# Last two element-wise steps of each spectral product on GpSimd, and a feed that aims eight steps ahead

## The chip, the core and the metric

One core of a Trainium2 chip runs the whole program. The metric is the device time of one execution in microseconds; lower is better. The engines are named as in the profile: PE is TensorE, PEld its weight load, DVE is VectorE, ACT is ScalarE, POOL is GpSimd, SP is SyncE. SP and POOL also issue DMAs, each from its own queue, in the order in which the instructions stand there.

## What is computed

A long convolution per channel, done with Fourier transforms, and a two-layer network on its result, all in float32:

```python
def _attn_ref(x, v, pos_emb, w1, w2):          # x, v: (4, 12480, 128)
    h_filt = (np.maximum(pos_emb @ w1, 0.0) @ w2) * window
    u = x * v
    y = irfft(rfft(u, n=2*S) * rfft(h_filt, n=2*S), n=2*S)[:, :S, :]
    return x * y
def _moe_ref(x, w_in, w_out):                  # x: (49920, 128), w_in: (128, 2048)
    h = x @ w_in
    g = h * (1.0 / (1.0 + np.exp(-1.702 * h)))
    return g @ w_out
```

## The kernel before

**Sets.** The convolution is cut into five sets (a half of the sequence, and one or two batch entries). A set has three phases. Phase 1 (`p1_unit`, 26 units) transforms the products x·v along one axis and stores them in DRAM as `g_d`. Phase 2 (`p2_unit`, 31 units a set, 30 of two columns and a last one of one) loads `g_d`, transforms along the other axis on PE (`forward`, L324, "cv<-g,wf"), multiplies by the filter's spectrum on DVE, transforms back on PE (`inverse`, L330, "ab<-t,wv") and stores `z_d`. Phase 3 (`p3_unit`) is done for each of 104 blocks of 480 columns: it loads `zt` (from `z_d`), `vt` and `x`, makes the last transform on PE (L520, "cv<-vt,zt"), and multiplies by x on DVE (L530 to L541). Set 0 goes through phases 1 and 2 in a start stage of about 200 us.

**The network.** After the start stage the program writes 104 blocks n of 8 steps k, that is 832 steps. A step has six matmuls of 480 columns into `h` (L592), two activations on ACT (L593, L594), one subtraction on DVE (L600, "fgl<-fg,fgh", written at the start of the next step) and six matmuls into `acc` (L609), three steps later. A block's result `ot` is stored from POOL at k = 4 of the next block (L620). At the end of step k = 7 of block n, `p3_unit(n + 2)` is started: its loads (L494 twice, L498, L500) are issued by POOL there, and its matmuls L520 are written at the end of step k = 2 of block n + 1, three steps later.

**The feed.** The phases 1 and 2 of sets 1 to 4 run between the steps. `Feed` holds their units with a weight each (1.4 or 1.6 for phase 1, 2.4 for phase 2) and marks, the summed weight at which a set is complete. After each step `feed.run(1.0)` raises a goal by a rate and lets units run until their weight has reached it. `feed.pace(k, span)` sets the rate to (mark − goal) / span. The rate is set at step 14 (`HOLD`) for set 1, and then at the steps 95, 199 and 407 (`begin`), at which the blocks of a new set are first loaded, for the sets 2, 3 and 4. Blocks 0 to 12 belong to set 0, 13 to 25 to set 1, 26 to 51 to set 2, 52 to 77 to set 3, 78 to 103 to set 4. So set 2 is prepared during the blocks of set 1, and so on; after set 4 is prepared only the network and phase 3 are left.

**The product.** Within a `p2_unit`, `t1` (called `y` in another view, two buffers) and `t2` (`yb`, one buffer) hold the products of the spectrum with the filter's real and imaginary part, in rows of 512 numbers a partition and half (256 in set 1 and in the last unit of a set). The sets 3 and 4 first add an older product (L419 or L423, L441, L443). The last two instructions, L463 and L464, form y = t1 − t2 and y = t1 + t2 on the two halves, in place. `inverse` reads y two or three units later. A `yield` ends a unit's share of one round, a `yield 1` only gives way to the steps.

Of the kernel before, what the change touches and what calls it, by code (L numbers as in the profile page):

```python
# [13 lines left out]
ALU = mybir.AluOpType  # L14
# [24 lines left out]
HOLD = 14  # L39
# [76 lines left out]
def conv_ffn_kernel(  # L116
# [17 lines left out]
    nc = tc.nc  # L134
    act = nc.scalar.activation
    tt = nc.vector.tensor_tensor
# [243 lines left out]
    def spec_store(eu, w0, nw, q=nc.sync):  # L380
        q.dma_start(out=e_d[0][:, w0:w0 + nw], in_=eu[:, 0, 0:nw])
        q.dma_start(out=us_d[0][:, 0, w0:w0 + nw], in_=eu[:, 1, 0:nw])

    def p2_unit(j, v):
# [27 lines left out]
        def tmp(name, bufs):  # L412
            t = sb(name, [128, 1024], F32, bufs)[:, 0:2 * wd]
            return t.rearrange("p (w l c) -> p w l c", w=nw, l=lq), t.rearrange("p (w l c) -> p w l c", w=nw, l=2)
# [19 lines left out]
        t1, y = tmp("t1", 2)  # L434
        t2, yb = tmp("t2", 1)
# [9 lines left out]
        else:  # L445
# [3 lines left out]
            if mixed:  # L449
                e1 = sb("e1", [128, 2, 2, 128], F32, 2)  # L450
                for i in range(2):
                    nc.vector.scalar_tensor_tensor(out=e1[:, 0:nw, i], in0=e0[:, 0:nw, i], scalar=sgn_sb,
                                                   in1=xs[i][:, :, 0], op0=ALU.mult, op1=ALU.add)
# [6 lines left out]
            yield 1  # L460
            tt(out=t2, in0=us[:, 0:nw], in1=both(e0, 1), op=ALU.mult)
            yield 1
        tt(out=y[:, :, 0], in0=y[:, :, 0], in1=yb[:, :, 1], op=ALU.subtract)  # L463
        tt(out=y[:, :, 1], in0=y[:, :, 1], in1=yb[:, :, 0], op=ALU.add)  # L464
        yield
        yield
        z = sb("z", [128, 2, 2, 256], F32, 3, "az")
# [155 lines left out]
    def conv_feed():  # L623
        p1 = {j: [(p1_unit(j, p), 1.6 if j == 1 else 1.4) for p in range(NP)] for j in range(1, 5)}
        ahead = {2: 5, 3: 16, 4: 16}
        units, marks = list(p1[1]), []
        for j in range(1, 5):
            nxt = p1.get(j + 1, [])
            n = ahead.get(j + 1, 0)
            units += nxt[:n]  # L630
            units += [(p2_unit(j, v), 2.4) for v in range(NV)]
            m = 8 if j == 1 else NP - n
            units += nxt[n:n + m]
            if j >= 3:
                units += [(None, 2.0)] * 12
            marks.append(sum(w for _, w in units))
            units += nxt[n + m:]
        return units, marks

    def fill(o, q):  # L640
        d = z_d[o][:, KZ:KP].rearrange("r k (q c) -> r (k q) c", c=128)
        q.dma_start(out=d, in_=zero.unsqueeze(1).broadcast_to([128, d.shape[1], 128]))

    with tc.manual_schedule():
# [48 lines left out]
        def when(n):  # L693
            return (n - 1) * STEPS - 1

        first = {next(i for i, hv in enumerate(HV) if hv[0] == o): o for o in range(1, 5)}
        begin = sorted(when(n) for n in first)
        feed = Feed(pipe, *conv_feed())
        feed.pace(0, begin[0] - HOLD)
        for n in range(7):  # L700
            p3.tick(p3_unit(n // 6) if n in (0, 6) else None)
            if n == 1:
# [8 lines left out]
        for n in range(NH):  # L711
            for k in range(STEPS):
                if pend:
                    ffn.lo(pend[-1])
                if len(pend) == LAG - 1 and pend[0][1] == STEPS - 1:
                    ffn.mm2(pend.pop(0))
                pend.append(ffn.mm1(n, k))
                t = n * STEPS + k
                if t == 1:
                    nc.gpsimd.tensor_tensor(out=sgn0, in0=gate[:, 0:1], in1=gate[:, 0:1], op=ALU.mult)  # L720
                if t == 1 or t == 9:
                    for _ in range(KEEP // 2):
                        spec_store(*spectra.pop(0), nc.gpsimd)
                if t == HOLD:
                    keep_cm.__exit__(None, None, None)
                    for o in range(1, 5):
                        fill(o, nc.gpsimd)
                    ps["s"] = ctx.enter_context(tc.tile_pool(name="main", bufs=1, side="right", reuse_waits="tile"))
                if len(pend) == LAG:
                    ffn.mm2(pend.pop(0))  # L730
                if t >= HOLD:
                    feed.run(1.0)
                new = None
                if k == STEPS - 1 and n + 2 < NH:
                    if n + 2 in first:
                        o = first[n + 2]
                        feed.reach()
                        if o < 4:
                            feed.pace(o, begin[o] - begin[o - 1] - 2)
                        else:  # L740
                            feed.rate = 0.0
                    new = p3_unit(n + 2)
                p3.tick(new)
                if k == 4:
                    ffn.store()
# [127 lines left out]
```

## Time and profile before

| | |
|---|---|
| time of the kernel before, median of 3 runs | 3049.63 us (3048.06 to 3049.92) |
| the profiled execution: its time, its span | 3054.41 us, 3052.6 us |
| mean granted TensorE clock | 0.994 |
| busy share of the span | PE 98%, PEld 77%, DVE 70%, ACT 69%, POOL 15% |
| instructions on POOL | 765 |
| DMA, mean over the span | 178 GB/s |

A row of the profile has line, engine, operation, the tile written and those read, the shapes as partitions × elements, the count, then busy microseconds and the mean time of one in nanoseconds, and then the engine's idle time just before them with what ended it. A row of the timeline has the start, the duration, and the same names. Busy DVE times of neighbours overlap a little: the spacing of starts is what one costs.

### The profile page before, as it was taken

The page shows a single profiled execution, that of the slowest core. Times are in us where ns is not written, and L with a number is a line of the kernel's source. Part 1 is how long each engine was busy: PE and PEld are TensorE (multiplying, and loading weights), DVE is VectorE, ACT ScalarE, POOL GpSimd, SP SyncE. Part 2 cuts the span into 40 slices and gives each one's busy share as a digit, 9 for nine tenths or more (in the row PEclk, how much of TensorE's full clock was granted, in tenths as well). Part 3 has the DMA queues.
Part 4 walks back from the last instruction along what each step waited for, and adds up shares of the span by engine and source line. Part 5 has one row for each costly group of instructions (what it writes and reads, how often), then busy time and mean ns, then how long its engine had stood idle before and what let it go on. Part 6 is the DMA issues. An engine that isn't in the chain of part 4 may idle for free.

```text
span 3052.6 us, 42552 instructions
## 1 busy us (share of the span) xinstructions
PE 2983.5 (98%) x15508; PEld 2349.7 (77%) x15508; DVE 2148.7 (70%) x2909; ACT 2091.3 (69%) x2689; POOL 466.7 (15%) x765
## 2 busy tenths in 40 slices
PE   8899999999999899999999999999999999999999
PEld 4458876688766688777778887777778888888888
DVE  7555677777787667999996469888995454444444
ACT  3456776688777777666668766666667677777676
POOL 2254111022101111101111111111111111111110
PEclk9999999999999999999999999999999999999999
DMA  9879899999788966666566324555541111111110
GB/s 298 265 256 285 243 292 281 290 315 312 248 269 270 277 187 203 200 197 195 189 190 172 112 83 158 170 163 165 177 142 63 57 50 46 60 46 46 60 46 27
DMA packets 261105, 541.88 MB, mean 178 GB/s; under 512 B 30978, under 2 KB 120762, under 8 KB 260898
## 3 DMA queue, kind: packets, MB, share of 16 engines
q1 hardware_dynamic: 205970, 377.29, 38.9%
q0 software_dynamic: 54928, 161.86, 17.7%
q8 instruction: 125, 2.05, 0.3%
q14 instruction: 82, 0.67, 0.1%
HBM read 330.24 MB, written 208.80 MB: 177 GB/s over the span
## 4 chain that ended last, share of the span: by engine, by line
PE 57%; DVE 7%; issue 1%; DMA 1%; ACT 0%; SPq 0%; POOL 0%; DVEq 0%; POOLq 0%
PE h L592 24%; PE acc L609 24%; PE cv L520 4%; DVE fgl L600 2%; PE ab L330 1%; DVE t L423 1%; PE cv L324 1%; DVE t L438 1%; DVE t L439 1%; DVE t L443 1%; PE cv L178 1%; PE cv L180 1%; PE cv L179 1%; DVE t L441 0%; DMA u<-us_d 0%
## 5 line engine op out<-in xcount | busy, mean ns | idle before, releaser
L600 DVE TENSOR_TENSOR fgl<-fg,fgh 128x960 fp32r<-128x960 f32 x832 | 956.9, 1154 | 426.0 <-ACT fg L594 424.3
L593 ACT ACTIVATE fgh<-h 128x960 fp32r<-128x960 f32 x832 | 809.1, 972 | 541.5 <-PE h L592 541.0
L592 PE MATMUL h<-xh,wi 128*128 128x480 f32 x3328 | 1149.4, 386 | 12.6 <-ACT fg L594 11.9
L609 PE MATMUL acc<-fgh,wo 128*128 128x480 f32 x3328 | 866.4, 382 | 0.0
L594 ACT ACTIVATE fg<-h 128x960 f32<-128x960 f32 x832 | 804.3, 967 | 65.3 <-DVE fgl L600 65.0
L592 PEld LDWEIGHTS h<-xh,wi 128*128 128x128 f32 x3328 | 628.0, 189 | 188.6 <-ACT fg L594 37.8
L609 PEld LDWEIGHTS acc<-fgh,wo 128*128 128x128 f32 x3328 | 625.8, 188 | 110.9 <-issue 12.9
L592 PE MATMUL h<-xl,wi 128*128 128x480 f32 x1664 | 634.3, 381 | 2.0 <-DVE xl L541 2.0
L609 PE MATMUL acc<-fgl,wo 128*128 128x480 f32 x1664 | 502.5, 383 | 5.2 <-DVE fgl L600 5.2
L620 POOL DMA_DIRECT2D out_dram<-ot x104 | 57.1, 549 | 1965.6 <-ACT ot L613 1908.9
L609 PEld LDWEIGHTS acc<-fgl,wo 128*128 128x128 f32 x1664 | 312.6, 188 | 57.4 <-DVE fgl L600 7.8
L592 PEld LDWEIGHTS h<-xl,wi 128*128 128x128 f32 x1664 | 313.8, 189 | 50.2 <-DVE xl L541 5.0
L520 PEld LDWEIGHTS cv<-vt,zt 122*128 122x128 f32 x1664 | 203.1, 194 | 28.9 <-issue 16.8
L520 PE MATMUL cv<-vt,zt 122*128 122x120 f32 x1664 | 207.6, 279 | 8.3 <-DMA vt<-in_c_v_dram 6.5
L324 PE MATMUL cv<-g,wf 52*64 52x512 f32 (+1 forms) x1240 | 178.9, 595 | 11.7 <-DMA g<-g_d 6.1
L530 DVE TENSOR_TENSOR a<-cv,yq 128x240 f32<-128x240 f32 (+1 forms) x101 | 40.7, 403 | 209.5 <-ACT yq L528 209.5
L494 POOL DMA_DIRECT2D zt<-z_d x204 | 148.4, 733 | 6.5 <-issue 3.7
L311 ACT ACTIVATE a<-cv 128x512 f32<-128x512 f32 x208 | 121.0, 599 | 17.2 <-PE cv L180 12.8
L473 ACT ACTIVATE z<-ab 128x1024 f32<-128x1024 f32 (+2 forms) x124 | 112.6, 908 | 28.7 <-PE ab L330 24.9
L278 POOL DMA_DIRECT2D ft<-in_c_f_dram x108 | 57.6, 535 | 451.9 <-PE cv L180 431.5
L330 PE MATMUL ab<-t,wv 52*64 52x512 f32 (+2 forms) x992 | 120.5, 556 | 1.2 <-ACT fg L594 1.2
L459 DVE TENSOR_TENSOR t<-us,e 128x512 f32<-128x512 f32 (+2 forms) x62 | 58.5, 944 | 86.3 <-PE ab L330 53.5
(90 smaller groups left out, 2561.9 us busy)
## 6 DMA issues: line engine op xcount, KB each, us to landing
g_d<-a SPq DMA_DIRECT2D x260, 256.0 KB
g<-g_d SPq DMA_DIRECT2D x300, 208.0 KB
zt<-z_d POOLq DMA_DIRECT2D x204, 256.0 KB, 4.7
e<-e_d SPq DMA_DIRECT2D x180, 256.0 KB
z_d<-z SPq DMA_DIRECT2D x90, 512.0 KB
xt<-in_xv_dram SPq DMA_DIRECT2D x78, 480.0 KB
u<-us_d SPq DMA_DIRECT2D x60, 512.0 KB
ft<-in_c_f_dram POOLq DMA_DIRECT2D x108, 240.0 KB, 5.1
```

Source lines behind the costliest of these rows:

```text
L311: act(a[:, ri], b, ACTF.Copy)
L324: mm(out=xy[q ^ c][64 * c:64 * c + 64, 0:256 * nw].rearrange("p (w c) -> p w c", w=nw), lhsT=wf[64 * q:64 * q + N2, c], rhs=g[64 * q:64 * ...
L330: mm(out=ab[h][64 * pl:64 * pl + 64, 0:w].rearrange("p (w c) -> p w c", w=nw), lhsT=wv[64 * h:64 * h + N2, pl], rhs=y[pl ^ h][64 * h:64 * ...
L459: tt(out=t1, in0=us[:, 0:nw], in1=both(e0, 0), op=ALU.mult)
L473: act(zv.rearrange("p w a c -> p a w c"), ab[:, :, 0:wd].rearrange("p a (w c) -> p a w c", w=nw), ACTF.Copy)
L494: q.dma_start(out=zv[:, gq], in_=z_d[o][64 * gq + 2 * p0:64 * gq + 2 * p0 + 2 * npr].rearrange("r k c -> k r c"))
L520: mm(out=b[:, c0:c0 + M], lhsT=lhs, rhs=rhs, start=(k == 0), stop=(k == 1))
L592: mm(out=h[:, i, 0:TW], lhsT=wt[:, s], rhs=xx, start=st, stop=sp)
L593: act(gh, h[:, :, 0:TW], ACTF.Gelu_apprx_sigmoid)
L594: act(gf, h[:, :, 0:TW], ACTF.Gelu_apprx_sigmoid)
L600: tt(out=gl, in0=gf, in1=gh.bitcast(F32), op=ALU.subtract)
L609: mm(out=acc, lhsT=wt[:, 2 * k + i, :], rhs=xx[:, i], start=(t == 0 and i == 0 and k == 0), stop=(t == 2 and i == 1 and k == STEPS - 1))
```

## The change

It moves the two last instructions of the product from VectorE to GpSimd, and it shortens each span over which the feed is paced by six steps, so that a set's mark is aimed at eight steps ahead of the step at which its first block is loaded instead of two (and for set 1 six steps earlier than before).

```diff
         tt(out=t2, in0=us[:, 0:nw], in1=both(e0, 1), op=ALU.mult)
         yield 1
-        tt(out=y[:, :, 0], in0=y[:, :, 0], in1=yb[:, :, 1], op=ALU.subtract)
-        tt(out=y[:, :, 1], in0=y[:, :, 1], in1=yb[:, :, 0], op=ALU.add)
+        pt = nc.gpsimd.tensor_tensor
+        pt(out=y[:, :, 0], in0=y[:, :, 0], in1=yb[:, :, 1], op=ALU.subtract)
+        pt(out=y[:, :, 1], in0=y[:, :, 1], in1=yb[:, :, 0], op=ALU.add)
         yield
...
         feed = Feed(pipe, *conv_feed())
-        feed.pace(0, begin[0] - HOLD)
+        feed.pace(0, begin[0] - HOLD - 6)
...
                         if o < 4:
-                            feed.pace(o, begin[o] - begin[o - 1] - 2)
+                            feed.pace(o, begin[o] - begin[o - 1] - 8)
```

The added line shifts the numbers behind it by one: L463 and L464 become L464 and L465, L494 becomes L495, L600 becomes L601 and so on.

The queue of POOL before, in the middle of set 2's phase 2, holds one block's store and the next but one block's loads, and nothing else:

```order
L500 DMA x_9483<-in_xtm_dram 128x480
L620 DMA out_dram<-ot 128x480
L494 DMA zt<-z_d_81 128x4x128 x2
L498 DMA vt<-in_c_v_dram 128x480
L500 DMA x_9783<-in_xtm_dram 128x480
```

The same place of POOL's queue in the changed kernel:

```order
L621 DMA out_dram<-ot 128x480
L464 TENSOR_TENSOR t_8867<-t_8867,t_8868 128x2x256
L465 TENSOR_TENSOR t_8867<-t_8867,t_8868 128x2x256
L464 TENSOR_TENSOR t_8937<-t_8937,t_8938 128x2x256
L465 TENSOR_TENSOR t_8937<-t_8937,t_8938 128x2x256
L495 DMA zt<-z_d_81 128x4x128 x2
L499 DMA vt<-in_c_v_dram 128x480
L501 DMA x_8978<-in_xtm_dram 128x480
```

Two pairs of the product now stand between the store and the loads, and the pair ahead of the loads reads t_8938, a tile that DVE writes.

The DVE order around that pair in the changed kernel, up to the phase 3 (a_9104) that uses the loads of x_8978:

```order
L459 TENSOR_TENSOR t_8937<-us,e_8793 128x1024
L461 TENSOR_TENSOR t_8938<-us,e_8793 128x1024
L601 TENSOR_TENSOR fgl<-fg,fgh 128x960 x2
L459 TENSOR_TENSOR t_9013<-us,e_8876 128x1024
L461 TENSOR_TENSOR t_9014<-us,e_8876 128x1024
L601 TENSOR_TENSOR fgl<-fg,fgh 128x960
L531 TENSOR_TENSOR a_9104<-cv,yq 128x240
L532 TENSOR_TENSOR a_9104<-cv,yq 128x240
```

Three subtractions of the network, so three steps, lie between t_8938 and L531 (L530 before): the pair is written in the very step at whose end the loads are issued.

In set 3 the DVE order before has L463 and L464 right behind L443, or one subtraction later:

```order
L441 TENSOR_TENSOR t_12442<-t_12442,t_12424 128x1024
L443 TENSOR_TENSOR t_12443<-t_12443,t_12427 128x1024
L463 TENSOR_TENSOR t_12442<-t_12442,t_12443 128x2x256
L464 TENSOR_TENSOR t_12442<-t_12442,t_12443 128x2x256
L600 TENSOR_TENSOR fgl<-fg,fgh 128x960 x2
L423 TENSOR_TENSOR t_12533<-u_12369,e_12367 128x4x128 x2
```

In the changed kernel DVE goes on with the network and the next unit's products:

```order
L441 TENSOR_TENSOR t_12462<-t_12462,t_12444 128x1024
L443 TENSOR_TENSOR t_12463<-t_12463,t_12447 128x1024
L542 TENSOR_TENSOR xl<-a_12397,xh 128x480
L601 TENSOR_TENSOR fgl<-fg,fgh 128x960 x2
L423 TENSOR_TENSOR t_12543<-u_12386,e_12384 128x4x128 x2
```

What follows L443 there reads two tiles in SBUF each time; the instructions that read PSUM (cv) come later.

## The prediction

> **What bounds the kernel now.** I read the page's first part, then windows from store to store in each stage, the groups, and last the timeline of POOL, DVE and PE around one phase 3. The page's first row:
>
> ```profile
> PE 2983.5 (98%) x15508; PEld 2349.7 (77%) x15508; DVE 2148.7 (70%) x2909; ACT 2091.3 (69%) x2689; POOL 466.7 (15%) x765
> ```
>
> PE looks full, but its ends are modelled, so I count blocks. The windows run from one `ot` (L613) to a later one: phase 2 of set 2 (from 829), of set 3 (1207), of set 4 (1830), and after the feed (2392). Columns: window, length, then PE, PEld, DVE, ACT, POOL busy with counts, granted clock, DMA share, GB/s.
>
> ```profile
> 829.40:987.30 157.90, 156.45 (x882) 107.89 (x881) 126.28 (x143) 119.97 (x156) 16.14 (x26) 1.00 0.81 267
> 1206.70:1605.50 398.80, 386.91 (x2064) 292.25 (x2063) 398.05 (x539) 257.13 (x302) 44.93 (x74) 1.00 0.61 193
> 1829.90:2245.60 415.70, 415.70 (x2193) 328.15 (x2192) 376.22 (x446) 282.73 (x331) 48.83 (x80) 1.00 0.51 166
> 2391.95:2801.55 409.60, 409.60 (x2018) 357.04 (x2017) 198.02 (x215) 288.72 (x342) 54.91 (x90) 1.00 0.16 51
> ```
>
> The same windows for L613 alone (both ends counted: blocks are the count less one), then for L330 (eight matmuls a unit):
>
> ```profile
> 829.40:987.30 157.90, 2.81 (x6) 1.00 0.81 267
> 1206.70:1605.50 398.80, 7.96 (x15) 1.00 0.61 193
> 1829.90:2245.60 415.70, 9.18 (x17) 1.00 0.51 166
> 2391.95:2801.55 409.60, 10.29 (x19) 1.00 0.16 51
> ...
> 829.40:987.30 157.90, 21.78 (x160) 4.15 (x160) 1.00 0.81 267
> 1206.70:1605.50 398.80, 32.67 (x240) 6.23 (x240) 1.00 0.61 193
> 1829.90:2245.60 415.70, 27.23 (x200) 5.20 (x200) 1.00 0.51 166
> ```
>
> A block without feed takes 409.60 / 18 = 22.76 us. In set 4, 16 blocks and 25 units take 415.70, so a unit adds (415.70 − 364.1) / 25 = 2.06 us of PE. Set 2 fits: 5 blocks and 20 units, 2.2 us a unit. In set 3, 14 blocks and 30 units should take 318.6 + 61.8 = 380.4 and take 398.8: some 18 us more, 3 of them for phase 1 units at the edges, and DVE is busy for 398.05 of 398.80. So PE is the bound in sets 2 and 4, where DVE has 20% and 9.5% to spare, and DVE in set 3, which costs 15 us. That is all that relief of DVE can bring there.
>
> **Part 1: the two instructions on GpSimd, as DVE sees them.** What leaves DVE, what such work costs on POOL (L365, L366 in the start stage), and what happens when both engines work at once:
>
> ```profile
> L463 DVE TENSOR_TENSOR t<-t,t 128x512 f32<-128x512 f32 x90 | 62.1, 690 | 2.1
> L464 DVE TENSOR_TENSOR t<-t,t 128x512 f32<-128x512 f32 x90 | 61.6, 685 | 0.0
> ...
> 195.29 0.72 POOL L366 TENSOR_TENSOR y<-t,t 128x256 f32<-128x256 f32 x1
> 195.97 0.45 POOL L365 TENSOR_TENSOR y<-t,t 128x128 f32<-128x128 f32 x1
> ...
> 147.98 1.29 DVE L361 TENSOR_TENSOR t<-cv,eu 128x512 f32<-128x512 f32 x2 [1.15 <-PE cv L330]
> 148.05 0.72 POOL L365 TENSOR_TENSOR y<-t,t 128x256 f32<-128x256 f32 x1 [1.02 <-PE cv L330]
> ...
> 165.31 0.68 DVE L564 TENSOR_TENSOR w<-w,w 128x512 uint32<-128x512 uint32 x1
> 165.55 1.01 POOL L365 TENSOR_TENSOR y<-t,t 128x256 f32<-128x256 f32 x1 [1.99 <-DVE t L361]
> 166.02 1.10 DVE L565 TENSOR_TENSOR w<-w,w 128x512 f32<-128x512 f32 x1
> 166.53 1.18 POOL L366 TENSOR_TENSOR y<-t,t 128x256 f32<-128x256 f32 x1
> 167.04 1.22 DVE L566 TENSOR_TENSOR w<-w,wo 128x512 f32<-128x512 f32 x1
> 168.29 0.69 DVE L567 SCALAR_TENSOR_TENSOR wo<-w,w 128x512 fp32r<-128x512 f32 x1
> ```
>
> From 128 to 256 numbers POOL goes from 0.45 to 0.72, so 512 cost about 0.72 + 0.55 = 1.27 us, against 0.69 on DVE. L361 reads PSUM, and neither side slows. L565 and L566 read two tiles in SBUF: they take 1.10 and 1.22 where their like takes 0.69, 0.41 and 0.53 more, while POOL's take 1.01 and 1.18 instead of 0.72. The engines take turns, and a GpSimd instruction of 0.72 us holds DVE up for 0.47. At 1.27 us I estimate 0.47 + 0.55 = 1.0; two a unit, 2.0, less a tenth because L438, L439, L530 and L531 read PSUM: 1.8. Relief is two starts, 1.21 us by the row spacing of L463 and L464 below (913.73 to 914.94). So DVE loses 0.6 us a unit instead of gaining 1.2.
>
> The Trainium skill ("SBUF — State Buffer", sections "SBUF: two separate sides" and "Who interferes with whom") says that GpSimd and a DVE instruction with two SBUF inputs exclude each other for the whole instruction. By that the loss would be 2 × 1.27 less a tenth, 2.3 a unit, and set 3 some 15 us slower than by the rows. The rows agree with the lock, but show it shorter than the instruction.
>
> Set 3 is DVE-bound: 31 × 0.6 = +19 us. Against it, the new pace runs set 3 at 0.625 weight a step instead of 0.642 (the goal has run past the mark by eight steps when the next span begins, so the shorter span is made up for): 2.6% more blocks, 0.4, in the stage, each with 12 us less DVE than PE work (198.02 / 18 = 11.0 against 22.8): −5. **Term 1: +14**, between −15 (no lock, DVE free) and +28 (each delay as long as POOL's 1.27). In sets 2 and 4 the 0.6 is covered by DVE's spare 20% and 9.5% (4 units of 31.6 us: 8%; 1.6 of 26 us: 4%); if that cover goes in set 4, +8, kept for the range.
>
> **Part 2: POOL's queue, where phase 3's loads stand.** Before, POOL waits for `ot`, stores, and goes straight on to the loads; nothing else is there:
>
> ```profile
> 893.39 1.50 POOL L494 DMA_DIRECT2D zt<-z_d  x2
> 894.88 0.55 POOL L498 DMA_DIRECT2D vt<-in_c_v_dram  x1
> ...
> 926.69 2.04 PE L520 MATMUL cv<-vt,zt 122*128 122x120 f32 x16
> ...
> vt<-in_c_v_dram POOLq DMA_DIRECT2D x6, 240.0 KB, 8.3
> ...
> vt<-in_c_v_dram POOLq DMA_DIRECT2D x14, 120.0 KB, 6.0
> ...
> 1059.40 1.47 POOL L494 DMA_DIRECT2D zt<-z_d  x2 [0.27 <-DMA g_d<-a]
> 1060.86 0.56 POOL L498 DMA_DIRECT2D vt<-in_c_v_dram  x1
> 1068.98 3.74 PE L520 MATMUL cv<-vt,zt 122*128 122x120 f32 x16 [4.04 <-DMA vt<-in_c_v_dram]
> ```
>
> vt is issued 31.8 us ahead of its use and lands in 8.3 (set 2; 6.0 in set 3). That lead exists because the loads, written at k = 7, run up to the store of k = 4. Where POOL's queue was held by other work (1059, behind phase 1 loads), vt had 8.1 us, PE stood 4.04 us, and the sixteen L520 then took 3.74 instead of 2.04: 5.7 us in all.
>
> With the change, L464 and L465 of one to three units stand between store and loads, and wait for DVE. The loads can't leave before the last pair is done. The DVE rows around that L520, to place it:
>
> ```profile
> 913.73 0.69 DVE L463 TENSOR_TENSOR t<-t,t 128x512 f32<-128x512 f32 x1
> 914.94 2.22 DVE L600 TENSOR_TENSOR fgl<-fg,fgh 128x960 fp32r<-128x960 f32 x2
> 922.27 1.15 DVE L600 TENSOR_TENSOR fgl<-fg,fgh 128x960 fp32r<-128x960 f32 x1
> 927.17 1.15 DVE L600 TENSOR_TENSOR fgl<-fg,fgh 128x960 fp32r<-128x960 f32 x1
> 930.70 0.40 DVE L530 TENSOR_TENSOR a<-cv,yq 128x240 f32<-128x240 f32 x1
> ```
>
> The loads stand three subtractions ahead of L530, so before the second one of 914.94. In the new order the pair's L459 and L461 come just there, behind the first: they end at about 918. Two GpSimd instructions of 1.27, each waiting for its turn, end at 921; two zt issues, 922.5; vt lands 8.3 later, 931. L520 is due at 926.7: PE stands 4 us, and its slow matmuls add 1.7 as at 1069. By the order of the changed kernel seven blocks of set 2 have the pair in the very step of the loads: 7 × 5.7 = **+40**, between 0 (products 4 us earlier) and +65.
>
> In set 3 three blocks have it in that step, six one step earlier. There:
>
> ```profile
> 1316.50 0.68 DVE L463 TENSOR_TENSOR t<-t,t 128x512 f32<-128x512 f32 x1
> 1322.37 1.94 PE L520 MATMUL cv<-vt,zt 122*128 122x120 f32 x16
> ```
>
> A pair ready at 1316.5 ends at 1320, zt at 1321.5, vt at 1327.5, 5 us after 1322.4; since DVE is the bound and works on behind PE, I take 3.5 of it: 3 × 3.5 = **+10**, and nothing for the others (one step is worth 3.5 us). Set 4: three such blocks, PE-bound, so 3.3 + 1.7 each: **+15**. Set 1 (half-size pairs, five such blocks): 1 us each, **+5**. These two are estimates from set 2's and set 3's rows, between 0 and twice that.
>
> Two waits are new on the tiles. t2 has one buffer, so the next unit's L461 (L439) waits for L465: in set 2 two subtractions and an L459 lie between, some 3.3 us, about what the pair takes, and in set 3 more; 0, or at most 0.5 us a unit in set 2, which PE's bound covers. `inverse` reads y two units later, 15 us in set 2 (31.6 / 4 each): 0.
>
> **Part 3: the earlier goal.** All issues of the units move with it: SP's loads and stores and POOL's ft keep their order among themselves, and the store and load queues see the same bytes. Set 1 runs 8% denser (134.2 weight in 75 steps, not 81). PE bounds that stage too, so the same work only moves: 0, or, if DMA should bound it (share 0.94 there at most), 0.4 of a block, +9. What it can bring is the stand at the end of set 2, where the last units come close together:
>
> ```profile
> 1019.25 0.49 PE L592 MATMUL h<-xh,wi 128*128 128x480 f32 x1 [3.86 <-ACT fg L594]
> ```
>
> With slow matmuls behind it, 1.7 as at 1069, it costs 5.6 us, and the late loads at 1069 another 5.7; at best both go. The units keep their order and only shift against the steps, so I take a third: **−4**, between −11 and 0.
>
> **Sum.** +14 + 40 + 10 + 15 + 5 − 4 = +80. The profiled execution took 3054.41 for a span of 3052.6, 4.8 over the median 3049.63; the terms are differences, so I add them to the median: 3130 us.
>
> **The rivals.**
> 1. POOL's delay is harmless (the products are early enough, or the landing is quicker when the queue is later): terms of part 2 vanish, +10 remain: 3060. For it: the 23 us between landing and use that the loads have before; against it: 1059.40, where the same lateness cost 5.7.
> 2. Faster: the engines hardly meet, because DVE's turns are long and POOL's short. Then set 3 becomes PE-bound, −15, and the stands at 1019 and 1069 go, −11: 3024. It decides if the delay per GpSimd instruction is under 0.6 us and part 2 adds nothing. Against it: L565 and L566.
> 3. The stalls feed on each other: DVE's delay makes the pairs later in set 4 too (four more blocks at 5 us) and set 2 takes its upper 65, set 4 its 8: +80 + 20 + 25 + 8: 3183.
>
> **How the numbers follow.** Forecast 0.58 (own range 3085 to 3170), rival 1 0.20, rival 2 0.10, rival 3 0.12. 0.2% of the time, 6 us, is about what a measurement of this kernel can tell. Slower: the forecast, rival 3 and most of rival 1, 0.85; same, 0.06 from between rivals 1 and 2; faster 0.09. The range leaves out rival 2 and the upper half of rival 3: 3052 to 3180.
>
> **What would show it.** L464 and L465 at about 1.3 us alone and up to 2 with waiting; L601 and L423 of set 3 with maxima near 2 us instead of 1.15 and 0.69; "PE cv L520 <- DMA vt" rising to tens of us; the loads in set 2 at most 12 us ahead of L520. If vt still leads by 20 us, part 2 is wrong; if set 3's blocks fall to 27.2 us, part 1 is.

## The result, and the profile after

| | before | after |
|---|---|---|
| median | 3049.78 us (4 runs) | 3158.80 us (4 runs, 3155.59 to 3164.79) |
| profiled execution: time, span | 3054.41, 3052.6 us | 3155.59, 3153.8 us |
| granted clock, mean | 0.994 | 0.98 |

The ratio is 1.0356 (95% interval 1.0343 to 1.0369): 109 us slower by the medians, 101 by the two profiled executions, from which the tables below are made. The first row of the page after:

```profile
PE 3016.5 (96%) x15508; PEld 2377.1 (75%) x15508; DVE 2144.9 (68%) x2661; ACT 2090.4 (66%) x2689; POOL 925.1 (29%) x1013
```

DVE has 248 instructions fewer and is busy for 3.8 us less (2148.7 before): what left came back as slower instructions. POOL's busy time doubled. The windows of the four stages of the feed show where the time lies. They run from the `ot` of block 0 to that of block 12, and on to the `ot` of blocks 25, 51 and 77, the last of each set; set 1 is prepared in the first, set 2 in the second, set 3 in the third, set 4 in the fourth (each but the last also holds about a block and a half of the next set's feed at its end). The columns are those of the prediction's windows. Before, and then after:

```profile
238.84:667.13 428.29, 419.11 (x2192) 320.91 (x2192) 306.22 (x540) 305.48 (x469) 75.51 (x128) 0.98 0.94 282
667.14:1097.72 430.58, 418.03 (x2178) 315.93 (x2178) 316.73 (x421) 328.30 (x446) 61.03 (x103) 0.98 0.86 270
1097.73:1801.66 703.93, 692.01 (x3559) 555.24 (x3559) 574.37 (x772) 486.78 (x595) 91.13 (x151) 1.00 0.57 174
1801.67:2460.14 658.47, 656.14 (x3409) 528.64 (x3409) 526.53 (x620) 448.62 (x524) 79.35 (x130) 1.00 0.41 134
```

```profile
237.72:684.84 447.12, 430.05 (x2243) 329.25 (x2243) 306.37 (x508) 315.87 (x492) 148.06 (x200) 0.98 0.96 291
684.85:1137.86 453.01, 422.95 (x2157) 321.31 (x2157) 310.30 (x348) 322.86 (x438) 171.96 (x161) 0.96 0.79 250
1137.87:1889.59 751.72, 705.97 (x3546) 564.60 (x3546) 579.13 (x703) 480.76 (x580) 245.04 (x210) 0.97 0.51 158
1889.60:2561.32 671.72, 658.78 (x3393) 532.58 (x3392) 525.09 (x545) 448.90 (x525) 199.96 (x190) 0.99 0.40 127
```

The stages lose 18.8, 22.4, 47.8 and 13.3 us; blocks 78 to 103 take 587.3 us in both. DVE is busy for 579 us in set 3 though 69 instructions fewer lie in that window. The list of waits (in total, times, longest) names what is new:

```profile
POOL t L464 <- DVE t L443: 586.4, 57, 32.9
PE cv L521 <- DMA vt<-in_c_v_dram: 74.6, 26, 7.2
PEld cv L521 <- DMA vt<-in_c_v_dram: 20.7, 5, 7.9
DVE t L439 <- POOL t L465: 13.9, 9, 1.8
```

PE waited 6.5 us in all for `vt` before. The 74.6 are 0.5 us in set 1, 24.9 in set 2, 36.3 in set 3 and 12.9 in set 4. The chain of work around one phase 3 of set 2 shows the step that the prediction worked out (start, duration, what):

```profile
891.97 2.08 POOL t L464
894.05 2.15 POOL t L465
896.20 1.46 POOL zt L495 x2
897.67 4.59 DMA vt<-in_c_v_dram
...
902.39 3.74 PE cv L521 x16
```

The pair takes 4.2 us instead of 2 × 1.25, the loads wait behind it, and `vt` is issued 4.7 us ahead of its use, late as that is, where it had 31.8. The timeline (start, duration, what, and in brackets the wait before) has the stand that follows (PE idle for 4.82 us) in its first row here. The other rows are from set 3, with two pictures of the meeting of the engines: at 1523 they take turns; at 1488 GpSimd ends only after DVE has left a gap:

```profile
902.39 3.74 PE L521 MATMUL cv<-vt,zt 122*128 122x120 f32 x16 [4.82 <-DMA vt<-in_c_v_dram]
...
1488.57 2.21 DVE L601 TENSOR_TENSOR fgl<-fg,fgh 128x960 fp32r<-128x960 f32 x2
1488.82 6.57 POOL L464 TENSOR_TENSOR t<-t,t 128x512 f32<-128x512 f32 x1 [10.45 <-DVE t L443]
1490.70 2.48 DVE L423 TENSOR_TENSOR t<-u,e 128x512 f32<-128x512 f32 x4
1493.11 1.14 DVE L601 TENSOR_TENSOR fgl<-fg,fgh 128x960 fp32r<-128x960 f32 x1
1494.89 0.69 DVE L438 TENSOR_TENSOR t<-cv,e 128x512 f32<-128x512 f32 x1 [0.64 <-PE cv L324]
1495.36 1.25 POOL L465 TENSOR_TENSOR t<-t,t 128x512 f32<-128x512 f32 x1
1496.64 0.69 DVE L439 TENSOR_TENSOR t<-cv,e 128x512 f32<-128x512 f32 x1 [1.05 <-POOL t L465]
1498.01 0.57 POOL L499 DMA_DIRECT2D vt<-in_c_v_dram  x1
1501.83 1.42 PE L521 MATMUL cv<-vt,zt 122*128 122x120 f32 x5 [7.00 <-DMA vt<-in_c_v_dram]
...
1522.80 1.15 DVE L601 TENSOR_TENSOR fgl<-fg,fgh 128x960 fp32r<-128x960 f32 x1
1523.05 2.04 POOL L464 TENSOR_TENSOR t<-t,t 128x512 f32<-128x512 f32 x1 [9.70 <-DVE t L443]
1523.87 2.24 DVE L601 TENSOR_TENSOR fgl<-fg,fgh 128x960 fp32r<-128x960 f32 x1
1525.06 2.20 POOL L465 TENSOR_TENSOR t<-t,t 128x512 f32<-128x512 f32 x1
1526.03 2.25 DVE L601 TENSOR_TENSOR fgl<-fg,fgh 128x960 fp32r<-128x960 f32 x1
...
1551.59 6.59 POOL L464 TENSOR_TENSOR t<-t,t 128x512 f32<-128x512 f32 x1 [11.03 <-PE h L593]
1564.85 3.74 PE L521 MATMUL cv<-vt,zt 122*128 122x120 f32 x16 [4.73 <-DMA vt<-in_c_v_dram]
```

In the case at 1488 PE then stands for 7.00 us, and L439 waits for L465, which still reads the one buffer of t2.

A stand costs more than its own length. The windows of the sixteen L521 behind the stand, and then of a sixteen without one in the kernel before:

```profile
902.39:906.13 3.74, 3.73 (x17) 3.74 (x18) 0.00 (x0) 0.00 (x0) 0.22 (x1) 0.50 0.95 362
```

```profile
926.69:928.73 2.04, 2.04 (x21) 2.04 (x18) 2.04 (x3) 1.96 (x4) 0.91 (x2) 1.00 0.98 289
```

The granted clock is 0.50 in the one and 1.00 in the other. So the 1.7 us that the prediction added to each stand are matmuls at half the clock. Each of the 14 stands of more than 2 us for `vt` in the sets 2 to 4 is followed by a slow sixteen, of 2.34 to 3.77 us.

### The profile page after: what moved, and what is told of

Its sections match the earlier page's. It is cut to its first block, busy times and chain, and to the rows that moved or that the text cites. A ratio compares the mean times of both kernels' runs of the same rounds, so it can differ in the third digit from the quotient of the medians.

```text
span 3153.8 us, 42690 instructions
## 1 busy us (share of the span) xinstructions
PE 3016.5 (96%) x15508; PEld 2377.1 (75%) x15508; DVE 2144.9 (68%) x2661; ACT 2090.4 (66%) x2689; POOL 925.1 (29%) x1013
## 4 chain that ended last, share of the span: by engine, by line
PE 33%; issue 24%; POOL 7%; DVE 7%; DMA 3%; ACT 0%; POOLq 0%; SPq 0%; DVEq 0%
PE h L593 13%; PE acc L610 12%; PE cv L521 4%; DMA vt<-in_c_v_dram 3%; POOL t L464 3%; DVE fgl L601 2%; POOL zt L495 2%; PE ab L330 2%; POOL t L465 1%; PE cv L324 1%; DVE t L438 1%; DVE t L439 1%; DVE t L443 1%; DVE t L423 1%; POOL out_dram L621 1%
## 5 line engine op out<-in xcount | busy, mean ns | idle before, releaser
L601 DVE TENSOR_TENSOR fgl<-fg,fgh 128x960 fp32r<-128x960 f32 x832 | 1050.9, 1269 | 428.5 <-ACT fg L595 422.6
L464 POOL TENSOR_TENSOR t<-t,t 128x512 f32<-128x512 f32 (+2 forms) x124 | 247.4, 1995 | 881.2 <-DVE t L443 586.4
L521 PE MATMUL cv<-vt,zt 122*128 122x120 f32 x1664 | 229.7, 297 | 76.8 <-DMA vt<-in_c_v_dram 74.6
L521 PEld LDWEIGHTS cv<-vt,zt 122*128 122x128 f32 x1664 | 222.7, 211 | 101.1 <-issue 68.0
L531 DVE TENSOR_TENSOR a<-cv,yq 128x240 f32<-128x240 f32 (+1 forms) x101 | 40.7, 403 | 287.1 <-ACT yq L529 287.1
L465 POOL TENSOR_TENSOR t<-t,t 128x512 f32<-128x512 f32 (+2 forms) x124 | 216.0, 1742 | 0.0
L495 POOL DMA_DIRECT2D zt<-z_d x204 | 149.9, 738 | 5.8 <-DMA zt<-z_d 2.8
```

Of the source, the lines that this page charges most:

```text
L464: pt(out=y[:, :, 0], in0=y[:, :, 0], in1=yb[:, :, 1], op=ALU.subtract)
L465: pt(out=y[:, :, 1], in0=y[:, :, 1], in1=yb[:, :, 0], op=ALU.add)
L495: q.dma_start(out=zv[:, gq], in_=z_d[o][64 * gq + 2 * p0:64 * gq + 2 * p0 + 2 * npr].rearrange("r k c -> k r c"))
L521: mm(out=b[:, c0:c0 + M], lhsT=lhs, rhs=rhs, start=(k == 0), stop=(k == 1))
L601: tt(out=gl, in0=gf, in1=gh.bitcast(F32), op=ALU.subtract)
```

## The experiments

"Before" in a ratio is the kernel before on the same chip. Four versions separate the parts first.

**The pace alone.** The changed kernel with the two instructions back on DVE:

```diff
-        pt = nc.gpsimd.tensor_tensor
-        pt(out=y[:, :, 0], in0=y[:, :, 0], in1=yb[:, :, 1], op=ALU.subtract)
-        pt(out=y[:, :, 1], in0=y[:, :, 1], in1=yb[:, :, 0], op=ALU.add)
+        tt(out=y[:, :, 0], in0=y[:, :, 0], in1=yb[:, :, 1], op=ALU.subtract)
+        tt(out=y[:, :, 1], in0=y[:, :, 1], in1=yb[:, :, 0], op=ALU.add)
```

> The changed pace with L463 and L464 left on VectorE. If the GpSimd queue and the shared port make the loss, the pace alone gives 3040 to 3055 us (the stand at the end of set 2 may go, at best 11 us). If the denser feed makes the loss, it gives 3080 or more.

Measured 3066.13 us, ratio 1.0048 (1.0031 to 1.0064), between the two ranges that were expected: a loss of some 15 us where the prediction had a gain. Its windows:

```profile
239.30:696.38 457.08, 432.49 (x2243) 329.03 (x2242) 321.08 (x570) 315.80 (x492) 81.22 (x138) 0.98 0.93 285
696.39:1117.44 421.05, 411.40 (x2157) 309.05 (x2156) 312.83 (x411) 322.56 (x438) 59.01 (x99) 1.00 0.85 268
1117.45:1817.50 700.05, 688.71 (x3546) 551.05 (x3546) 576.37 (x767) 480.87 (x580) 88.40 (x146) 1.00 0.55 169
1817.51:2470.62 653.11, 653.10 (x3393) 528.47 (x3392) 514.51 (x605) 449.00 (x525) 79.47 (x130) 1.00 0.41 131
```

The gains at the end of set 2 and behind are there (−9.5, −3.9, −5.4; block 23 takes 32.9 us instead of 44.0, block 25 28.3 instead of 35.5), but the denser set 1 costs +28.8. PE has 13.4 us more work in that window, which the three later ones are spared (−6.6, −3.3, −3.0), so the work only moves; the other 15.4 us are new idle time of PE, and they make the loss.

**GpSimd alone**, with the old pace:

```diff
-        feed.pace(0, begin[0] - HOLD - 6)
+        feed.pace(0, begin[0] - HOLD)
...
-                            feed.pace(o, begin[o] - begin[o - 1] - 8)
+                            feed.pace(o, begin[o] - begin[o - 1] - 2)
```

> The two instructions on GpSimd with the old pace (two steps ahead). If the loss comes from GpSimd, 3140 to 3170 us, as the whole change, since the pairs still stand between store and loads. If the pace is half of it, about 3100.

3128.85 us, ratio 1.0249 (1.0232 to 1.0266), which is neither of the two times expected. By the ratios the two instructions alone cost 76 us and the pace alone 15; together they cost 109, so some 18 belong to both at once (each of the three is known to 4 or 5 us). PE waits 48.7 us for `vt` here and 74.6 in the change: the pace seems to decide, too, which pairs stand ahead of the loads.

**The loads ahead of the pairs.** The changed kernel with phase 3's loads written at k = 4, right behind the store, and three more yields, so that L521 stays in its step; 3 instead of 6 and 5 instead of 8 in the pace, since `begin` counts from the loads:

```diff
-                if k == STEPS - 1 and n + 2 < NH:
+                if k == 4:
+                    ffn.store()
+                if k == 4 and n + 2 < NH:
...
```

> The whole change, but phase 3's loads are written three steps earlier, at k = 4 right behind the store, so that no pair of k = 5 to 7 stands ahead of them; L521 stays where it is. Queue theory: the waits of PE for vt fall from over 100 us to under 20, and the time to 3060 to 3085; what is left over the twin without GpSimd is what VectorE loses by the shared port, 15 to 30 us. Port theory (VectorE held up is the main loss, the late vt a symptom): 3110 or more.

**Its twin on DVE**, the same without GpSimd's instructions:

> The twin of the one above with L463 and L464 on VectorE: the loads at k = 4, the pace eight steps ahead. 3035 to 3050 us: the loads behind phase 1's ft get three steps more, which can take the stand of 5.7 us at 1069 and a few like it. Its difference to the run above is the price of GpSimd with a free queue.

The first gave 3081.99 us, ratio 1.0098 (1.0082 to 1.0114), 77 less than the change. PE's wait for `vt` is no longer in its list, while L439's wait for L465 is longer:

```profile
DVE t L439 <- POOL t L465: 25.3, 14, 2.1
```

The twin gave 3057.12 us, ratio 1.0017 (1.0006 to 1.0028), slower than the 3035 to 3050 expected. The early loads thus take 9 us off the pace alone, and what GpSimd still costs with its loads out of the way is 25.

**The loads on another queue.** Since the loads at k = 4 also come earlier in the program, a later run left them where the change has them and took them off POOL:

```diff
-        q = nc.gpsimd if n > 1 else nc.sync
+        q = nc.sync
```

> The changed kernel whole, but phase 3's loads (zt, vt, x) are issued by SP at the end of step 7, as late as they are written, so that they no longer stand behind the two GpSimd instructions; POOL keeps the stores. If the loss of 77 us that went with the loads at k = 4 comes from their place in POOL's queue, and not from the later steps of phase 3, most of it goes here too: 3085 to 3110, with the vt waits of PE under 20 us together and a lead of vt near 20 us. Rival: what counts is only how early the loads are written; SP too issues them at k = 7, behind its own loads and stores of the feed, and the time stays at 3140 to 3165.

3089.31 us, ratio 1.0122 (1.0108 to 1.0136): in the first range, so the place in the queue is what costs. Its windows, and from its list of waits the one for `vt`:

```profile
238.54:694.52 455.98, 431.71 (x2243) 331.38 (x2243) 305.78 (x508) 316.21 (x492) 111.39 (x146) 0.97 0.94 285
694.53:1118.76 424.23, 412.31 (x2157) 312.30 (x2157) 310.40 (x349) 322.62 (x438) 138.44 (x109) 0.99 0.84 265
1118.77:1840.31 721.54, 695.54 (x3546) 554.36 (x3545) 575.83 (x703) 480.22 (x580) 196.83 (x106) 0.99 0.53 164
1840.32:2493.42 653.10, 653.09 (x3393) 528.48 (x3392) 526.47 (x545) 448.93 (x525) 135.06 (x86) 1.00 0.41 132
```

```profile
PE cv L521 <- DMA vt<-in_c_v_dram: 14.6, 9, 2.6
```

With these the 102 us of the four windows fall into three parts, each the difference of two of the runs above:

| stage | change − before | pace (pace alone − before) | GpSimd, loads out of its queue (loads on SP − pace alone) | the queue (change − loads on SP) | predicted |
|---|---|---|---|---|---|
| set 1 | +18.8 | +28.8 | −1.1 | −8.9 | +5 |
| set 2 | +22.4 | −9.5 | +3.2 | +28.8 | +40 − 4 |
| set 3 | +47.8 | −3.9 | +21.5 | +30.2 | +19 − 5 + 10 |
| set 4 | +13.3 | −5.4 | 0.0 | +18.6 | +15 |
| sum | +102.3 | +10.0 | +23.6 | +68.7 | +80 |

**What on GpSimd holds DVE.** Two runs on the loads at k = 4. In the first GpSimd only writes zeros into `y`:

```diff
-        pt = nc.gpsimd.tensor_tensor
-        pt(out=y[:, :, 0], in0=y[:, :, 0], in1=yb[:, :, 1], op=ALU.subtract)
-        pt(out=y[:, :, 1], in0=y[:, :, 1], in1=yb[:, :, 0], op=ALU.add)
+        for i in range(2):
+            nc.gpsimd.memset(y[:, :, i], 0.0)
```

> As the run with the two instructions on GpSimd and the loads at k = 4, but GpSimd only writes zeros into the two halves of y and reads nothing (the subtraction and addition are left out). Port theory (GpSimd's reads hold VectorE): VectorE is free and relieved, 3040 to 3057 us against 3082, and L601 in set 3 keeps its 1.15 us. Theory of the added waits (PE and VectorE wait for GpSimd's queue): near 3075.

In the second DVE does all the work, and GpSimd multiplies `y`, in pieces of 256 numbers, into a scratch tile that nobody reads:

```diff
+        for i in range(2 * nw):
+            scr = sb("scr", [128, 2, 128], F32, 1)[:, 0:nq]
+            nc.gpsimd.tensor_tensor(out=scr, in0=y[:, i // 2, i % 2].rearrange("p (q c) -> p q c", q=nq),
+                                    in1=zero.unsqueeze(1).broadcast_to([128, nq, 128]), op=ALU.mult)
```

> The twin with L463 and L464 on VectorE and the loads at k = 4 (3057 us), and besides GpSimd multiplies the pieces of y (256 numbers each, two inputs in SBUF) into a scratch tile that nothing reads: the same GpSimd work, no relief, nobody waits for it. Port theory: four holds of some 0.47 us a unit, 1.9 us, 31 units of the VectorE-bound set 3: 3100 to 3125 us. Theory of the added waits: 3055 to 3062.

3047.79 us, ratio 0.9979 (0.9967 to 0.9991), in its range, and 3153.75 us, ratio 1.0333 (1.0316 to 1.035), above the 3100 to 3125 expected: set 3 loses 52.5 us on the twin on DVE, near the four holds of 0.47 a unit, but the sets 1, 2 and 4 lose 13.1, 15.0 and 12.5 more, which were not counted. Set 3 in the windows of the two (704.40 us in the twin on DVE):

```profile
1115.21:1802.15 686.94, 686.15 (x3552) 551.93 (x3552) 540.36 (x707) 481.09 (x583) 119.31 (x211) 1.00 0.56 174
```

```profile
1138.70:1895.56 756.86, 707.73 (x3552) 559.27 (x3552) 629.95 (x771) 480.99 (x583) 277.71 (x273) 0.98 0.50 157
```

And the network's subtraction, grouped from 1250 to 1550 us, with zeros written, and then with the reads:

```profile
L604 DVE TENSOR_TENSOR fgl<-fg,fgh 128x960 fp32r<-128x960 f32 x89 | 101.2, 1152 | 0.0
```

```profile
L608 DVE TENSOR_TENSOR fgl<-fg,fgh 128x960 fp32r<-128x960 f32 x76 | 101.5, 1347 | 0.0
```

Relief without reads is worth 17.5 us in set 3, and PE takes over as the bound (686.15 of 686.94). The zeros read neither `y` nor t2, so this run takes away the holding and DVE's wait for t2 together. The second has the holding alone: no engine waits for its scratch work in set 3, and yet four instructions a unit whose result nobody needs cost (756.86 − 704.40) / 31 = 1.69 us a unit, 0.42 each. So it is GpSimd's reading that holds DVE, not its being busy. The Trainium skill ("SBUF — State Buffer", section "Who interferes with whom") says that a DVE instruction with two inputs in SBUF contends with a GpSimd instruction that reads SBUF and not with one that only writes it: 1152 ns against 1347 agree.

**The two paces apart**, both without GpSimd, each against the pace alone: set 1 at the old pace and the later sets eight steps ahead; then set 1 at the new pace and the later sets at two.

```diff
-        feed.pace(0, begin[0] - HOLD - 6)
+        feed.pace(0, begin[0] - HOLD)
```

> No GpSimd; the pace eight steps ahead for the sets 2 to 4, the old one for set 1. The pace alone lost 29 us in the blocks 1 to 12, where set 1 is fed 8% denser, and gained 19 behind. If the density in that stage is the loss, 3035 to 3050 us; if the gain behind came only from work moved ahead into set 1's stage, 3050 to 3062.

```diff
-                            feed.pace(o, begin[o] - begin[o - 1] - 8)
+                            feed.pace(o, begin[o] - begin[o - 1] - 2)
```

> No GpSimd; the old pace for the sets 2 to 4, six steps less for set 1. If the density in set 1's stage is the loss, 3065 to 3080 us; if the later spans are, about 3050.

3039.70 us, ratio 0.9958 (0.9946 to 0.997), and 3062.59 us, ratio 1.0035 (1.0017 to 1.0053); the first is in the range for the density of set 1's stage, the second 2.4 us below it. The earlier goal helps the later sets (696.0 and 653.1 us instead of 703.9 and 658.5) and hurts set 1 (457.5 instead of 428.3); the first of the two beats both kernels.

**What more can be had without GpSimd.** On the first of the two, the loads at k = 4 except those of a set's first block; then the twelve empty entries at the ends of the sets 3 and 4 made lighter, which gives the real units more steps; then both:

```diff
-                if k == STEPS - 1 and n + 2 < NH:
+                if k == 4:
+                    ffn.store()
+                if k == (STEPS - 1 if n + 2 in first else 4) and n + 2 < NH:
...
```

> No GpSimd work; set 1 at its old pace, the later sets eight steps ahead (pace_set1_old, 3039.7), and the loads written at k = 4, except for the first block of a set. If the earlier loads bring something by themselves (the loads at k = 4 took 9 us off pace_only), 3030 to 3036; if what they brought there was a stand that the old pace of set 1 does not have, 3038 to 3042.

```diff
-                units += [(None, 2.0)] * 12
+                units += [(None, 0.8)] * 12
```

> No GpSimd work; pace_set1_old with the twelve empty entries at each end of a set weighing 0.8 instead of 2.0, so that the feed's real work is spread over more steps of sets 2 to 4. Set 3 is bound by VectorE at 27 to 28 us a block while its last blocks run at 22.8: spreading its 31 units over two more blocks takes some 10 us off it, 3025 to 3035. Rival: the lighter ends bring phase 1's last stores later against the first block that loads them, and PE stands at blocks 23 and 49: 3040 to 3055.

> Both: loads at k = 4 and the lighter empty entries. If the two add, 3020 to 3030; if either brings stands at a set's first block, 3035 to 3055.

3039.79 us (0.9956, 0.9942 to 0.997): the early loads add nothing here, where set 1 has its old pace. 3031.02 us (0.993, 0.9917 to 0.9943) with the lighter entries, and 3029.05 us (0.9925, 0.9912 to 0.9937) with both, which the runs don't tell apart. Sets 3 and 4 with the lighter entries:

```profile
1094.25:1782.27 688.02, 685.19 (x3546) 550.66 (x3546) 571.29 (x759) 479.56 (x579) 88.30 (x146) 1.00 0.55 171
1782.28:2435.83 653.55, 653.37 (x3393) 528.49 (x3392) 519.75 (x611) 448.74 (x525) 79.34 (x130) 1.00 0.41 132
```

688.0 us, 8.0 less than with the old weights, is within 1.1 us of what full relief of DVE gave set 3 (686.9): spreading the same work over more blocks brought set 3 to where the two instructions were to bring it, without a second engine.

## Why the prediction was right, and where it was off

The forecast was 3130 us and slower; 3158.8 lies in its own range. The mechanism of the largest term holds, and the 29 us that are missing (22 in the profiled executions) are mainly one step of part 3.

**Part 2, the queue: right; that its sum fits too is partly luck.** +70 predicted, 69 measured (77 by the version with early loads, which bring 9 without GpSimd too). The block of set 2 at 902 went as worked out: a stand of 4 us and matmuls slower by 1.7 predicted, 4.82 and 3.74 − 2.04 = 1.70 found. `vt` landed in 4.6 us instead of the 8.3 that I took, but the pair took 4.2 instead of 3. Of the 68.7 us, 25.1 are PE's longer busy time (2217.75 us in the four windows against 2192.65), as the slow matmuls behind the stands make it. The division among the sets was off. In set 2 six blocks stand behind a pair, three for nearly 5 us and three for 1.8 to 1.9, where seven of 4 were counted. Its size depends on the run it is set against: +28.8 against the loads on SP, where a few short waits remain, and +39.7 against the early loads (453.01 − 413.35). Set 3 lost 27 to 30 instead of 10: the three blocks with the pair in the step of the loads stood for 14.5 us together (3.5 each counted), but I costed the blocks with the pair a step or more ahead at nothing, "one step is worth 3.5 us", and these stood for the other 21.8 of the 36.3: at 1551.59 a single L464 of 6.59 us ate that step. Set 1 gained 9 to 12 us by the late loads, where a loss of 5 was predicted; why is open. Set 4 lost 16 to 19 against 15, and its three blocks stood for 3.3 to 3.7 us, as counted.

**Term 1, port and relief: right in size, partly by luck and for another reason.** In set 3 +19 was predicted for the port against the relief, and 20.0 (early loads, 724.43 − 704.40) or 21.5 (loads on SP) were measured; sets 2 and 4 cover it, as said. The bound of −15 for relief without a lock was −17.5. But I had the whole loss as holding of DVE, 1.8 us a unit, and costed the wait on t2's single buffer at 0. DVE's busy time in set 3 is the same with and without the two instructions (575.83 us with the loads on SP, 576.37 with the pace alone), so the holding takes about what the relief gives: 35.5 us, or 1.1 a unit, over the 540.36 of the run that writes zeros. Where the engines take turns, at 1523, one GpSimd instruction makes a DVE instruction 1.1 us longer, near the 1.0 that I took; but a starved L464 as at 1488 doesn't lengthen DVE's, and the average is 0.6. L439 waits for L465 for 22.3 us in set 3 with the loads on SP and for 25.3 with the early loads, and that is about the net loss. So two wrong terms, a holding that was too large and a wait that was left out, came to the right sum. That is read from the traces; a second buffer for t2, which would tell the two apart, was not tried.

**Part 3, the pace: wrong in sign.** −4, with −5 more in term 1, against +10 in the profiled executions and +15 by the medians. The step that failed is "PE bounds that stage too, so the same work only moves: 0". The work did only move, but PE idled 15.4 us more in set 1. What the pace was to bring at the end of set 2 came about nearly as priced: PE idles 2.9 us less in set 2 (430.58 − 418.03 against 421.05 − 411.40; −4 predicted). Set 3 is 3.9 us shorter where term 1 had −5, but 3.3 of that is PE work that now lies in an earlier window (692.01 − 688.71); PE idles only 0.6 us less, so the relief that was meant isn't shown. The value that I kept for the case that DMA bounds that stage, +9, was the nearer one. For that case speaks that the window moves 8% more (285 × 457.08 against 282 × 428.29) at the same rate in 6.7% more time, and that PE's waits there for the transfers of `g` and `pt` grow from 2.5 us each to 8.2 and 8.0, 11.2 of the 15.4. No run varied the transfers of set 1 alone, so this is argued, not shown.

**The rivals.** The first (the delay is harmless) fell with PE's wait for `vt`, 74.6 us instead of 6.5. The second (the engines hardly meet) fell with L601: 1.35 us in the middle of set 3 instead of 1.15. The third, 3183, is partly true: the pieces that feed each other, a starved L464 that makes the loads late, are there, but eight of the ten L464 of more than 4 us lie in set 3's window, and the other two at the very start of set 4's. The signs that I had named came: loads in set 2 4.7 us ahead of L521, and these maxima (min/median/max in ns; L601, L423, L464):

```profile
L601 DVE TENSOR_TENSOR fgl<-fg,fgh x832: 1136/1157/2257, 214.6 to 3145.2; 128x960 fp32r<-128x960 f32 x167
L423 DVE TENSOR_TENSOR t<-u,e x124: 410/678/1776, 1206.0 to 1647.8; 128x512 f32<-128x512 f32 x120, 128x256 f32<-128x256 f32 x4
L464 POOL TENSOR_TENSOR t<-t,t x124: 726/1584/7743, 410.5 to 2383.3; 128x512 f32<-128x512 f32 x90, 128x256 f32<-128x256 f32 x33, 128x128 f32<-128x128 f32 x1
```

The last goes far beyond the 2 us that I had named.

## What to carry to other kernels

Before work goes to an engine that also issues DMAs, list what stands behind it in that engine's queue: here two small instructions a unit cost 69 us by the loads behind them, and 24 by themselves. An engine that waits for a late producer passes the wait on to every load written after it, so issue the loads first or from a queue that doesn't wait for that producer. And when one stage is bound by one engine, first see whether its work can be spread into blocks that have room: that brought 8 us in set 3 for a change of one weight.

## What the hardware showed that was not expected

- The turns between DVE and GpSimd are not fair. At 1523 they alternate: L464 ends 1.14 us after the first L601, the next L601 1.02 after that, L465 1.15 after that and the last L601 1.02 later still, so each does nearly all of its own length (1.25 and 1.15 us) only when the other has ended. The prediction's rows of the start stage, where it read a lock shorter than the instruction, show the same: each ends 0.55 to 0.59 us after the other, of lengths of 0.69 and 0.72. At 1488 L464 starts as far behind an L601 as at 1523, 0.25 us, but waits on through six more DVE instructions with two inputs in SBUF, which run at their usual length, and ends 1.14 us after the last of them: 6.57 us in all, and up to 7.74 elsewhere. What decides between the two was not found. The Trainium skill ("SBUF — State Buffer", section "SBUF: two separate sides") says that whichever of the two starts first gets the pair of ports for the whole instruction, and the other blocks. That it is for the whole instruction agrees with both cases; that the first to start gets it doesn't hold at 1488, where six instructions that started after L464 went ahead of it.
- A GpSimd instruction that only writes SBUF (525 ns for 512 numbers, 180 times) left DVE's two-input instructions at 1152 ns; one that reads held them by 0.42 us a piece of 256.
